# One-hot transposes of an attention and MLP kernel: both heads of a pair at once, 128 output rows in place of 64

## The chip, the cores and the metric

The kernel runs on one core of one Trainium2 chip. The metric is device time in microseconds (us) of one execution. Executions of the same kernel scatter by about 0.3 us and more, so most of what follows is read from traces, where the same instruction can be compared to within some 0.02 us.

## The reference, cut to what matters

Four batches of eight heads, 768 tokens, head size 64. Each query and key is assigned to the nearest of 16 centroids; a query attends to the keys of the same cluster only; then comes softmax, the product with v, and a GELU MLP.

```python
q_assign = np.argmax(np.einsum('bhsd,hcd->bhsc', q_n, c_n), axis=-1)
k_assign = np.argmax(np.einsum('bhsd,hcd->bhsc', k_n, c_n), axis=-1)
mask = q_assign[:, :, :, None] == k_assign[:, :, None, :]
scores = np.where(mask, scale * np.matmul(q, k.transpose(0, 1, 3, 2)), -1e9)
# softmax, then @ v;   x = that, heads side by side
# out = gelu(x @ w_in) @ w_out,  x: (3072, 512), w_in: (512, 2048)
```

## The kernel before

The mask enters the score product as 16 more rows of the contraction: the one-hot of the cluster (minus 1 on the key side, times a large number on the query side). So for each head the kernel needs q, k and both one-hots transposed. For heads 0 to 9 TensorE makes these transposes, for the later heads a DMA. In order, for one head: q transposes and their copy out by DVE, k transposes and copy, assignment products on TensorE, sum, maximum and comparison on DVE (the one-hot, [token, cluster]), one-hot transposes on TensorE, and two evictions by DVE into rows 64 to 79 of the transposed q and k.

```python
ps_sc = ...tile_pool(name="ps_sc", bufs=2, space=PSUM)   # scores
ps_a  = ...tile_pool(name="ps_a",  bufs=1, space=PSUM)   # assignment products
ps_x  = ...tile_pool(name="ps_x",  bufs=1, space=PSUM)   # attention times v
ps_o  = ...tile_pool(name="ps_o",  bufs=2, space=PSUM)   # all transposes of heads 0 to 9
# ... cut ...
ohs = [const.tile([128, N, 2, 2, 32], FP16, name=f"oh{t}") for t in range(NOH)]  # [token, chunk, head of pair, q/k, 32]
for t in ohs:
    nc.vector.memset(t[:, :, :, :, 16:32], 0.0)

def tr_pe(i, w, copy=None, pool=None):                  # w = 0: q, 1: k
    # ... cut ...
    for j in range(N):
        nc.tensor.transpose(t_ps[:, j * 128:(j + 1) * 128], st[:, w, j, :], ident)     # line 154
    (copy or nc.vector.tensor_copy)(Ts[i][:, w, :], t_ps)                              # line 155

def one_pe(i):
    oh = ohs[(i // 2) % NOH]
    e = i % 2
    t_ps = ps_o.tile([128, S], FP16, tag="op", name="oh_ps")
    for j in range(N):
        nc.tensor.transpose(t_ps[0:64, j * 128:(j + 1) * 128],
                            oh[:, j, e].rearrange("p b c -> p (b c)"), ident)          # line 265
    nc.vector.tensor_scalar(Ts[i][D:D + C, 1, :], t_ps[32:32 + C, :], -1.0, None, op0=ALU.add)          # 267
    nc.vector.tensor_scalar(Ts[i][D:D + C, 0, :], t_ps[0:C, :], float(VAL), None, op0=ALU.mult)         # 269
# ... cut: one_first, the same for head 0 in two halves (line 287) ...
AVS0 = {2: (0,), 3: (1, 2), 4: (3,), 5: (4, 5)}   # products with v after score chunk 2, 3, ...
def slot(i, c):                        # score chunk c of head i, c = 0 to 5
    scores(i, c)                       # 2 matmuls (line 311), 1 exponential on ACT (line 314)
    # ... products with v of head i-1 (line 326); after chunk 5 its normalization (336, 337)
# program order: g(i, c) is just after score chunk c of head i
        at(g(h - 2, 0), tr_pe, h, 0)
        at(g(h - 2, 2), tr_pe, h, 1)
        at(g(h - 2, 4), prep_asn, h, True)        # products 219, sum 232, maximum 239, one-hot 240
        at(g(h - 1, 1), one_pe, h)
    # x_tok of an even head and the next, transposed (350) and copied (352):
        at(g(h + 3, 3), fin, h, pe=True)
```

The pairs (i, c) show what shares a head's time: while head i is scored, head i+2 is transposed and assigned, and head i+1's one-hot is transposed.

The softmax here doesn't subtract the row's maximum and nothing guards it: scores larger than these inputs give would overflow.

## Time and profile before

| | before |
|---|---|
| time, median (range) of 3 runs | 302.98 us (302.97 to 303.14) |
| span of the profiled execution | 301.14 us |
| from the start to the first MLP product of line 386 (FC1 in the prediction) | 55.70 us |
| one pair of heads (two in a row, out of heads 3 to 7) | 9.71 us |

Three stages matter: a start of 8 us (loads, head 0), heads 0 to 9 with hardly any MLP work (eight products of one early tile), and from 55.7 us on a TensorE-bound rest of 245.4 us. The change touches the first two.

The page of the kernel before: busy time by engine, and the chain that ended last.

```profile
PE 296.4 (98%) x3109; PEld 186.0 (62%) x3109; DVE 121.7 (40%) x284; ACT 216.0 (72%) x274; POOL 106.8 (35%) x182
...
## 4 chain that ended last, share of the span: by engine, by line
PE 97%; ACT 1%; DVE 1%; issue 0%; DVEq 0%
```

The windows view over one pair of heads (28.66 to 38.37 us, from one sum on DVE to the same one two heads later); columns as in its first line.

```profile
core 0: us, PE busy (x) PEld busy (x) DVE busy (x) ACT busy (x) POOL busy (x), PEclk, DMA share, GB/s
28.66:38.37 9.71, 9.71 (x164) 7.51 (x163) 8.68 (x20) 9.29 (x13) 9.30 (x15) 1.00 1.17 266
```

PE is busy in all of it, then POOL, ACT, and DVE last. A matmul's busy time runs to its modelled end, which lies after the start of the next, so PE's 9.71 of 9.71 hides waits; they must be read from start-to-start distances. PE's row around one one-hot group (start us, us, engine, line, operation, out<-in, forms, count), in head 4:

```profile
29.86 0.49 PE L311 MATMUL sc_ps<-T 80*128 80x384 f16 x2
30.27 0.52 PE L265 MATMUL oh_ps<-ident,oh_167 128*64 128x128 f16 x6
30.73 0.50 PE L311 MATMUL sc_ps<-T 80*128 80x384 f16 x2
31.06 0.35 PE L326 MATMUL x_ps<-vaug_148,p_sb 128*128 128x65 f16 x6
31.25 0.50 PE L154 MATMUL tr_ps<-ident,st 128*128 128x128 f16 x6
```

`128*64` is the array form: 128 rows, 64 weight columns. The group starts 0.41 us after the first score matmul in front of it, where the plain sequence needs 0.16 (to the second score matmul) plus 0.16. Its weight loads, minimum/median/maximum ns, from the view of line 265:

```profile
L265 PEld LDWEIGHTS <-oh_166 x24: 106/110/110, 17.2 to 49.9; 128*64 128x64 f16 x24
```

DVE's row for the same head, from one one-hot to the next sum:

```profile
29.65 0.35 DVE L240 TENSOR_TENSOR oh_167<-asum,asn_ps 128x192 f16<-128x192 f32 x1
29.92 0.19 DVE L336 RECIPROCAL rec<-x_ps 128x6 f32<-128x6 f32 x1
30.14 0.56 DVE L337 TENSOR_TENSOR x_tok<-x_ps,rec 128x384 f16<-128x384 f32 x1
30.62 0.55 DVE L155 COPY T<-tr_ps 128x768 f16<-128x768 f16 x1
31.20 0.55 DVE L267 TENSOR_SCALAR T<-oh_ps 16x768 f16<-16x768 f16 x1
31.76 0.55 DVE L269 TENSOR_SCALAR T<-oh_ps 16x768 f16<-16x768 f16 x1
32.34 0.56 DVE L155 COPY T<-tr_ps 128x768 f16<-128x768 f16 x1
33.31 0.56 DVE L232 TENSOR_REDUCE asum<-asn_ps 128x192 f32<-128x384 f32 x1 [0.41 <-PE asn_ps L219]
```

In every second head, where x_tok is transposed as well, it looks like this (lines of both engines):

```profile
36.41 0.55 DVE L269 TENSOR_SCALAR T<-oh_ps 16x768 f16<-16x768 f16 x1
...
37.02 0.51 PE L350 MATMUL fin_ps<-ident,x_tok 128*128 128x128 f16 x6
...
37.88 0.45 PE L219 MATMUL asn_ps<-c_all,T 128*128 128x32 f16 x12
...
38.37 0.56 DVE L232 TENSOR_REDUCE asum<-asn_ps 128x192 f32<-128x384 f32 x1 [0.24 <-PE asn_ps L219]
```

And the clearing of the last one-hot buffer, with DVE's next instruction:

```profile
1.30 0.22 DVE L124 MEMSET oh_167<- 128x192 uint32 x1
3.26 0.36 DVE L162 CAST st<-q_raw 128x384 f16<-128x384 f32 x1 [1.75 <-DMA q_raw<-in_q_dram]
```

### The profile page before, as it was taken

The page shows a single profiled execution, that of the slowest core. Times are in us where ns is not written, and L with a number is a line of the kernel's source. Part 1 is how long each engine was busy: PE and PEld are TensorE (multiplying, and loading weights), DVE is VectorE, ACT ScalarE, POOL GpSimd, SP SyncE. Part 2 cuts the span into 40 slices and gives each one's busy share as a digit, 9 for nine tenths or more (in the row PEclk, how much of TensorE's full clock was granted, in tenths as well). Part 3 has the DMA queues.
Part 4 walks back from the last instruction along what each step waited for, and adds up shares of the span by engine and source line. Part 5 has one row for each costly group of instructions (what it writes and reads, how often), then busy time and mean ns, then how long its engine had stood idle before and what let it go on. Part 6 is the DMA issues. An engine that isn't in the chain of part 4 may idle for free.

```text
span 301.1 us, 7413 instructions
## 1 busy us (share of the span) xinstructions
PE 296.4 (98%) x3109; PEld 186.0 (62%) x3109; DVE 121.7 (40%) x284; ACT 216.0 (72%) x274; POOL 106.8 (35%) x182
## 2 busy tenths in 40 slices
PE   8899999999999999999999999999999999999996
PEld 4577777666666666666566666666566665565444
DVE  5788987103564742122353742213344413000112
ACT  5889999956888888856788888855788883466000
POOL 3999999997034104572633104600000000000000
PEclk9999999999999999999999999999999999999999
DMA  6999999994369348966679436876032242100122
GB/s 219 341 297 274 264 263 202 240 197 131 63 176 218 81 99 224 199 187 157 134 175 185 119 82 209 165 97 131 2 89 53 71 52 46 38 0 0 44 97 70
DMA packets 74065, 42.85 MB, mean 142 GB/s; under 512 B 54320, under 2 KB 71088, under 8 KB 74032
## 3 DMA queue, kind: packets, MB, share of 16 engines
q1 hardware_dynamic: 69520, 38.09, 53.4%
q0 software_dynamic: 4224, 4.19, 8.3%
q8 instruction: 24, 0.39, 0.5%
q10 hardware_dynamic: 288, 0.10, 0.1%
q14 instruction: 9, 0.07, 0.1%
HBM read 27.30 MB, written 6.29 MB: 112 GB/s over the span
## 4 chain that ended last, share of the span: by engine, by line
PE 97%; ACT 1%; DVE 1%; issue 0%; DVEq 0%
PE hp L386 27%; PE op L412 24%; PE sc_ps L311 21%; PE x_ps L326 11%; PE op_alt L412 3%; PE asn_ps L219 3%; PE tr_ps L154 2%; PE w_ps L98 1%; PE oh_ps L265 1%; ACT p_sb L314 1%; PE fin_ps L350 1%; PE asn_ps L223 0%; PE hp_early L367 0%; DVE T L269 0%; DVE T L267 0%
## 5 line engine op out<-in xcount | busy, mean ns | idle before, releaser
L314 ACT ACTIVATE p_sb<-sc_ps 128x768 f16<-128x768 f32 x192 | 149.7, 810 | 21.3 <-PE sc_ps L311 12.8
L311 PE MATMUL sc_ps<-T 80*128 80x384 f16 x384 | 93.8, 325 | 0.6 <-ACT p_sb L314 0.4
L386 PE MATMUL hp<-xt,w_in_sb 128*128 128x384 f16 x504 | 85.0, 326 | 0.0
L326 PEld LDWEIGHTS <-p_sb 128*128 128x128 f16 x1152 | 54.7, 97 | 30.8
L386 PEld LDWEIGHTS <-w_in_sb 128*128 128x128 f16 x504 | 47.9, 98 | 30.4
L132 POOL CAST st<-q_raw 128x384 f16<-128x384 f32 x30 | 15.4, 513 | 78.9 <-DMA q_raw<-in_q_dram 57.3
L416 DVE COPY o_sb<-op 128x512 f32<-128x512 f32 (+1 forms) x22 | 14.8, 672 | 55.0 <-PE op L412 54.9
L232 DVE TENSOR_REDUCE asum<-asn_ps 128x192 f32<-128x384 f32 x29 | 16.2, 558 | 50.8 <-PE asn_ps L219 50.7
L311 PEld LDWEIGHTS <-T 80*128 80x128 f16 x384 | 26.2, 97 | 5.8 <-issue 0.9
L133 POOL TENSOR_TENSOR st<-q_raw,st 128x384 f16<-128x384 f32 x30 | 27.3, 911 | 2.4
L135 POOL TENSOR_TENSOR st<-k_raw,st 128x384 f16<-128x384 f32 x30 | 27.4, 912 | 2.4
L336 DVE RECIPROCAL rec<-x_ps 128x6 f32<-128x6 f32 x32 | 6.2, 193 | 43.8 <-PE x_ps L326 43.8
L337 DVE TENSOR_TENSOR x_tok<-x_ps,rec 128x384 f16<-128x384 f32 x32 | 17.8, 558 | 1.1
L219 PEld LDWEIGHTS <-T 128*128 128x128 f16 x348 | 14.6, 96 | 4.4
L219 PE MATMUL asn_ps<-c_all,T 128*128 128x32 f16 x348 | 16.5, 177 | 0.0
L134 POOL CAST st<-k_raw 128x384 f16<-128x384 f32 x30 | 15.1, 505 | 0.0
L275 DVE TENSOR_SCALAR T<-ohT 16x768 f16<-16x768 f16 x22 | 7.9, 361 | 8.0 <-DMA ohT<-oh_166 3.6
L239 DVE TENSOR_REDUCE asn_ps<-asum 128x12 f32<-128x192 f32 x29 | 10.5, 361 | 1.0
L154 PE MATMUL tr_ps<-ident,st 128*128 128x128 f16 x120 | 10.6, 228 | 0.2 <-DVE T L269 0.2
L154 PEld LDWEIGHTS <-st 128*128 128x128 f16 x120 | 8.2, 101 | 2.9 <-DVE st L163 0.8
L155 DVE COPY T<-tr_ps 128x768 f16<-128x768 f16 x17 | 9.4, 554 | 0.6
L278 DVE TENSOR_SCALAR T<-ohT 16x768 f16<-16x768 f16 x22 | 8.6, 391 | 0.3
(308 smaller groups left out, 404.8 us busy)
## 6 DMA issues: line engine op xcount, KB each, us to landing
q_raw<-in_q_dram SPq DMA_DIRECT2D x32, 192.0 KB, 4.1
k_raw<-in_k_dram SPq DMA_DIRECT2D x32, 192.0 KB, 4.1
v_raw<-in_v_dram SPq DMA_DIRECT2D x32, 192.0 KB, 4.4
out_dram<-o_sb SPq DMA_DIRECT2D x23, 256.0 KB, 2.2
w_in_sb<-in_moe_w_in_dram POOLq DMA_DIRECT2D x4, 512.0 KB, 10.4
w_out_sb<-in_moe_w_out_dram POOLq DMA_DIRECT2D x4, 512.0 KB, 11.9
T<-st SPq DMA_TRANSPOSE x22, 4.9
xt<-x_tok SPq DMA_TRANSPOSE x11, 2.9
```

The costliest lines, as they stand in the source:

```text
L132: nc.gpsimd.tensor_copy(st[:, 0, :, 0:D], q_raw)
L133: nc.gpsimd.tensor_sub(st[:, 0, :, D:2 * D], q_raw, st[:, 0, :, 0:D])
L135: keng.tensor_sub(st[:, 1, :, D:2 * D], k_raw, st[:, 1, :, 0:D])
L154: nc.tensor.transpose(t_ps[:, j * 128:(j + 1) * 128], st[:, w, j, :], ident)
L219: nc.tensor.matmul(a_ps[:, j, which], t[:, js], c_all[:, :, chs], start=True, stop=True)
L232: nc.vector.tensor_reduce(out=asum, in_=a_ps.rearrange("p n w l c -> p n w c l"), axis=AX.X, op=ALU.add)
L311: nc.tensor.matmul(s_ps[:, t, 0:QB], Ts[i][0:D + C, 1, c * 128:(c + 1) * 128], Ts[i][0:D + C, 0, t * QB:(t + 1) * QB], start=True, stop=True)
L314: nc.scalar.activation(ps[i][:, c, :].rearrange("p (t q) -> p t q", t=2), s_ps[:, :, 0:QB], ACT_FN.Exp, bias=0.0, scale=float(scale))
L326: nc.tensor.matmul(x_ps[:, j], ps[i][:, ch, j * 128:(j + 1) * 128], va[:, ch, 0:D + 1], start=(ch == 0), stop=(ch == N - 1))
L337: nc.vector.tensor_tensor(xtoks[i - i % 2][:, :, i % 2, :], x_ps[:, :, 0:D], rec.to_broadcast([128, N, D]), op=ALU.mult)
L386: nc.tensor.matmul(hp[:, t, 0:QB], w_in_sb[:, m, f * 128:(f + 1) * 128], xts[b][:, m, t * QB:(t + 1) * QB], start=(m == 0), stop=(m == NM ...
L412: nc.tensor.matmul(op[:, 0:w], gs[b][f][:, js], w_out_sb[:, f, ms], start=(f == 0), stop=(f == NF - 1))
```

## The change

Its intent: weight loads and transposes of 64 columns put TensorE in another array form and back, ten times. With both heads of the pair taken at once the form stays 128x128. The other head's rows are computed and not read, so its buffer must hold something: the clearing covers all of it.

```diff
-        nc.vector.memset(t[:, :, :, :, 16:32], 0.0)
+        nc.vector.memset(t, 0.0)
@@ one_pe
-            nc.tensor.transpose(t_ps[0:64, j * 128:(j + 1) * 128],
-                                oh[:, j, e].rearrange("p b c -> p (b c)"), ident)
-        nc.vector.tensor_scalar(Ts[i][D:D + C, 1, :], t_ps[32:32 + C, :],
+            nc.tensor.transpose(t_ps[:, j * 128:(j + 1) * 128],
+                                oh[:, j].rearrange("p a b c -> p (a b c)"), ident)
+        nc.vector.tensor_scalar(Ts[i][D:D + C, 1, :], t_ps[64 * e + 32:64 * e + 32 + C, :],
                                 -1.0, None, op0=ALU.add)
-        nc.vector.tensor_scalar(Ts[i][D:D + C, 0, :], t_ps[0:C, :],
+        nc.vector.tensor_scalar(Ts[i][D:D + C, 0, :], t_ps[64 * e:64 * e + C, :],
                                 float(VAL), None, op0=ALU.mult)
# ... cut: the same two lines for head 0
```

More of the change, by code (lines that the diff above doesn't have):

```diff
@@ L286, in one_first @@
             for j in range(N // 2):
-                nc.tensor.transpose(t_ps[0:64, j * 128:(j + 1) * 128],
-                                    ohs[0][:, e * (N // 2) + j, 0].rearrange("p b c -> p (b c)"),
+                nc.tensor.transpose(t_ps[:, j * 128:(j + 1) * 128],
+                                    ohs[0][:, e * (N // 2) + j].rearrange("p a b c -> p (a b c)"),
                                     ident)
```

## The prediction

> **What bounds the kernel.** The page's chain that ended last is 97% PE; PE is busy 98%, ACT 72%, DVE 40%. The affected stage is the first 56 us (heads 0 to 9); after it the chain is pure PE, so an earlier start should pass through one to one. In the first stage PE and ACT take turns. By the windows view, between 20 and 55 us ACT is busy 4.6 to 4.9 of each 5 us, PE 4.8 to 5.0. Exponentials back to back start 0.70 us apart (0.805 us each, overlapping 0.10), so ACT alone would need 4.2 us a head; the heads take 4.65 (no x_tok transpose) or 5.06 us (with one). Most steps wait for PE; one, the second score chunk of each head, waits for ACT (it starts 0.05 us after the exponential two before it ends).
>
> **What the change does.** No instruction is added or removed; order and semaphore waits stay. Ten groups of six one-hot transposes go from a 128x64 to a 128x128 array form. The matmuls stream the same 128 columns: 56 ns apart inside a group, as the 128x128 transposes of q and k (line 154), so the doubled output rows are free. The load of 64 weight columns takes 110 ns, that of 128 columns 97 to 101. What goes is at the edges. Start-to-start distances, one-hot group against line-154 group:
> - last score matmul to first transpose: 253 ns against 161;
> - first to second transpose: 80 against 55 to 59;
> - last transpose to next matmul: 152 against 56;
> - first to second score matmul after it: 173 against 162 to 167.
> That is about 0.21 us a group, 1.9 us over nine. The Trainium skill, "TensorEngine Tiling (Array Packing)", Key Properties, says that changing the tiling mode drains TensorE, and under Restrictions that column tiling disables fast weight load; both fit (line-154 weight loads start before the previous matmul is through, those of the one-hots only with their matmul).
>
> The memsets of the three one-hot buffers write twice the elements (0.22 us each before; I estimate 0.3 to 0.45) and end by about 2.1 us; DVE then waits for q_raw until 3.26: hidden. The evictions read the same 16 rows at another partition: no change.
>
> **How much is on the path.** The group follows chunk 1 of a head; chunk 2's scores wait for the exponential of chunk 0. They start 162 to 169 ns after it ends; the floor seen elsewhere is 51. So heads 4 to 8 give only about 0.115 each, not 0.21: 0.58. Head 2's group has 0.7 us of room: 0.20. Head 3: 0.14 (it waits for the one-hot, mainly the exit counts). Head 1: 0.11, through DVE's wait for it. Head 9: 0.06, chunk 3 already waits for ACT. Head 0: 0.03. Sum about 1.1 us.
>
> **Prediction:** 302.98 - 1.1 = 301.9 us, 301.2 to 302.6 eight times in ten. Faster by over 2%: 0.5%; within 2%: 99%; slower: 0.5%.
>
> **What would show it.** One-hot groups as 128*128, weight loads near 100 ns; entry near 161, exit near 56 ns or longer where it waits for ACT; chunk 2's scores 51 ns after the exponential; head pairs at 9.47 us instead of 9.70; FC1 starting at about 54.7 us instead of 55.86, everything later shifted equally. Memsets longer, still done before q_raw lands.
>
> **What would make it wrong.** If the edges come not from the array form but from waits on DVE or the PSUM buffer, nothing is gained (302.9). If ACT's floor moves too, up to 1.9 us (301.1). If a later stage is paced by a DMA or POOL (95% busy until 67 us), the gain is given back there.

## More of the kernel before

Every run was with a granted TensorE clock of 1.0 or 0.999.

From 29.65 to 32.90 us DVE goes from instruction to instruction without a wait, and takes up the one-hot transposes (line 267) at 31.20, while PE had started the last of them at 30.58 (30.27 plus 0.08 plus four times 0.056). Then comes one gap of 0.41 us before line 232.

## The result, and the profile after

| | before | after |
|---|---|---|
| first measurement, median (range) | 303.00 us (302.97 to 303.14), 4 runs | 302.75 us (302.68 to 302.94), 4 runs |
| its ratio | | 0.9992, 95% interval 0.9975 to 1.0009 |
| second measurement | 302.95 us (302.90 to 303.46), 9 runs | 302.95 us (302.62 to 303.13), 5 runs |
| its ratio | | 0.9995, 95% interval 0.9983 to 1.0008 |

A ratio is the mean time of one kernel's runs over that of the other's of the same rounds, so not quite the ratio of the medians. Both intervals hold 1: end to end, the gain of 0.0 to 0.25 us is not clear of the noise. The traces are clearer. From the first exponential to the end the kernel before takes 291.25 us, the changed one 291.03 and 290.99 in two profiles: 0.23 to 0.26 us less. The 1.1 us forecast did not come.

The same views after. The page:

```profile
PE 295.8 (98%) x3109; PEld 186.8 (62%) x3109; DVE 122.8 (41%) x284; ACT 215.2 (72%) x274; POOL 106.6 (35%) x182
...
## 4 chain that ended last, share of the span: by engine, by line
PE 94%; POOL 2%; DVE 1%; ACT 1%; issue 0%
```

One pair of heads (28.50 to 38.23 us, the same two sums):

```profile
28.50:38.23 9.73, 9.73 (x164) 7.86 (x163) 8.70 (x20) 9.07 (x13) 9.32 (x15) 1.00 1.16 255
```

PE around the same group, and the weight loads:

```profile
29.70 0.48 PE L311 MATMUL sc_ps<-T 80*128 80x384 f16 x2
30.02 0.50 PE L265 MATMUL oh_ps<-ident,oh_167 128*128 128x128 f16 x6
30.45 0.48 PE L311 MATMUL sc_ps<-T 80*128 80x384 f16 x2
30.78 0.34 PE L326 MATMUL x_ps<-vaug_148,p_sb 128*128 128x65 f16 x6
31.06 0.49 PE L154 MATMUL tr_ps<-ident,st 128*128 128x128 f16 x6
```

```profile
L265 PEld LDWEIGHTS <-oh_166 x24: 95/97/100, 17.1 to 49.7; 128*128 128x128 f16 x24
```

The form is now `128*128`, and the edges that the prediction named are gone, except the exit: from the last transpose to the next score matmul it is 150 ns, was 152, and this is now a wait for an exponential. First score matmul to first one-hot transpose: 0.32 us, was 0.41. But look at the last line of this view, before and after: from the start of the products with v (line 326) to the k transposes (line 154) it took 0.19 us before and takes 0.28 now. PE arrives earlier and waits. What for is in DVE's row:

```profile
30.46 0.55 DVE L155 COPY T<-tr_ps 128x768 f16<-128x768 f16 x1
31.04 0.56 DVE L267 TENSOR_SCALAR T<-oh_ps 16x768 f16<-16x768 f16 x1
31.62 0.56 DVE L269 TENSOR_SCALAR T<-oh_ps 16x768 f16<-16x768 f16 x1
32.20 0.56 DVE L155 COPY T<-tr_ps 128x768 f16<-128x768 f16 x1
33.17 0.56 DVE L232 TENSOR_REDUCE asum<-asn_ps 128x192 f32<-128x384 f32 x1 [0.41 <-PE asn_ps L219]
```

Line for line it is the row of before, shifted by 0.14 to 0.16 us: the copy of q, the two evictions, the copy of k, and the same gap of 0.41 us. DVE's copy of q (line 155) ends at 31.012 us, and PE's k transposes, which need its buffer, start 0.05 us later. Before, it ended at 31.165 and PE came 0.085 us later: PE had 0.035 us to spare there. The pair of heads takes 9.73 us, was 9.71.

In the head with x_tok, too, the rows follow each other as before, the x_tok transposes right after the end of the second eviction (36.82 us here, 36.96 before):

```profile
36.27 0.55 DVE L269 TENSOR_SCALAR T<-oh_ps 16x768 f16<-16x768 f16 x1
36.88 0.51 PE L350 MATMUL fin_ps<-ident,x_tok 128*128 128x128 f16 x6
...
38.23 0.56 DVE L232 TENSOR_REDUCE asum<-asn_ps 128x192 f32<-128x384 f32 x1 [0.24 <-PE asn_ps L219]
```

A ledger from the traces, in us, each stretch between the starts of two exponentials (3.0 is chunk 0 of head 3) or from there to the first MLP product of line 386:

| stretch | before | after | after, second profile |
|---|---|---|---|
| start to head 0's one-hot | 8.171 | 8.225 | 8.112 |
| 0.0 to 2.0 | 9.905 | 9.587 | 9.583 |
| 2.0 to 3.0 | 4.906 | 5.026 | 5.026 |
| 3.0 to 8.0 | 24.465 | 24.503 | 24.482 |
| 8.0 to 9.2 | 5.919 | 5.848 | 5.855 |
| 9.2 to the first MLP product | 0.618 | 0.633 | 0.633 |
| from there to the end | 245.441 | 245.429 | 245.411 |

The gain is made in heads 0 and 1 (0.32), a part is given back in head 2 (0.12), heads 3 to 7 give nothing, and heads 8 and 9 give 0.07. The first of these repeats in all profiles: 9.905 to 9.913 us in the six kernels with 64 columns in heads 0 to 2, 9.583 to 9.590 in the nine with 128.

What PE's time became, in the pair of heads 5 and 6: summing what the start-to-start distances exceed the normal ones (0.162 us for 384 columns streamed, 0.056 for 128, 0.029 for 65, 0.025 for 32), before there were 0.44 us of edges of the one-hot groups among 0.78 us in all; after there are no such edges and 0.80 us in all, of which 0.25 are waits for exponentials (0.06 before) and 0.22 waits before the k transposes (none before). The edges turned into waits.

The clearing takes longer and is hidden, as forecast:

```profile
1.73 0.38 DVE L124 MEMSET oh_167<- 128x384 uint32 x1
3.33 0.36 DVE L162 CAST st<-q_raw 128x384 f16<-128x384 f32 x1 [1.22 <-DMA q_raw<-in_q_dram]
```

### The profile page after: what moved, and what is told of

Read it like the earlier page. It is cut to its first block, busy times and chain, and to the rows that moved or that the text cites. A ratio compares the mean times of both kernels' runs of the same rounds, so it can differ in the third digit from the quotient of the medians.

```text
span 300.9 us, 7413 instructions
## 1 busy us (share of the span) xinstructions
PE 295.8 (98%) x3109; PEld 186.8 (62%) x3109; DVE 122.8 (41%) x284; ACT 215.2 (72%) x274; POOL 106.6 (35%) x182
## 4 chain that ended last, share of the span: by engine, by line
PE 94%; POOL 2%; DVE 1%; ACT 1%; issue 0%
PE hp L386 27%; PE op L412 24%; PE sc_ps L311 20%; PE x_ps L326 11%; PE op_alt L412 3%; PE asn_ps L219 3%; PE tr_ps L154 2%; PE w_ps L98 1%; PE oh_ps L265 1%; PE fin_ps L350 1%; POOL st L133 1%; ACT p_sb L314 1%; ACT T L155 1%; PE hp_early L367 0%; POOL st L132 0%; POOL st L135 0%
## 5 line engine op out<-in xcount | busy, mean ns | idle before, releaser
L275 DVE TENSOR_SCALAR T<-ohT 16x768 f16<-16x768 f16 x22 | 8.2, 371 | 8.2 <-DMA ohT<-oh_166 4.0
L278 DVE TENSOR_SCALAR T<-ohT 16x768 f16<-16x768 f16 x22 | 9.0, 410 | 0.3
```

## The experiments

Theory A: in heads 3 to 8 DVE, taking its instructions in order, and PE release each other in a loop that the one-hot group is not part of. Rival B: the prediction's own mechanism, the exponentials on ACT as the floor, only mis-sized. The times below are device times; "3.0 to 8.0" is the stretch of the ledger, 24.465 us in the kernel before and 24.48 to 24.50 in the changed one. All results were accepted as correct.

### w0to2: the change for heads 0 to 2 alone

```diff
+        wide = i < 3          # else as before, in 64 columns
```

> The change for heads 0, 1 and 2 alone (all three buffers cleared whole as in the change). Theory A (in heads 3 to 8 DVE, working through its instructions in order, sets the pace, and the one-hot group on PE is not in that loop): nearly the whole gain of the change remains, 302.70 to 302.80 us; in the trace the start of the q/k transposes is 0.15 to 0.18 us earlier than in the kernel before from head 3 on and stays so to head 8 (no loss per pair, because the evictions of the odd heads read from the low partitions again); a pair of heads 9.70 us. Rival B (ACT's exponentials absorb what PE gains, as the prediction's floor says, and only the size is off): less gain than the whole change, because heads 3 to 9 are missing, with the shift growing from head to head in the changed kernel and not here.

Measured: 302.98 us median (302.57 to 303.16), ratio 0.9994 (0.9980 to 1.0008). The time missed the range: in this profile head 0's one-hot came at 8.46 us, 0.29 later than before, in the start that the change hardly touches. From the first exponential to the end it took 291.01 us, 0.24 less than before, which is the whole gain of the full change; 3.0 to 8.0 took 24.454. As theory A has it.

### w3to9: the change for heads 3 to 9 alone

```diff
+        wide = i >= 3         # head 0 in 64 columns too
```

> The change for heads 3 to 9 alone. Theory A: no gain in heads 3 to 8 although each of their groups is 0.2 us shorter on PE: 302.9 to 303.05 us; the q/k transposes shift by 0 from head 3 and then 0.016 us later with every odd head (its two evictions from the high partitions take 10 and 6 ns longer); a pair of heads 9.70 to 9.72 us; PE's gaps before the second q/k group of each head about 0.10 us longer. The prediction on record would have 302.1 to 302.3 here.

Measured: 302.97 us median (302.88 to 303.73), ratio 1.0003 (0.9991 to 1.0016). 3.0 to 8.0 took 24.491 us, 0.026 more than before, although five groups in it are shorter on PE. From the first exponential to the end 291.21 us, 0.05 less, which heads 8 and 9 gave (5.849 against 5.919). This alone rules out the 0.58 us that were predicted for the groups of heads 4 to 8, which lie in this stretch.

### b_nosum and a_nosum: DVE's sum left out for heads 3 to 9, in both kernels

A wrong result (the maximum that follows goes to SBUF and no longer to PSUM, cut here): the cluster is chosen from the high halves of the centroids alone, so 0.558 us a head of DVE go and PE's work stays.

```diff
-            asum = small.tile(...); nc.vector.tensor_reduce(out=asum, in_=..., op=ALU.add)
+            if i < 10:
+                asum = a_ps[:, :, :, 0, :]
```

> Kernel before, but for heads 3 to 9 the one-hot is made from the high halves alone: the sum of the two halves on DVE (0.558 us a head) is left out. Wrong result on purpose (a few assignments flip), same PE work. Theory A: DVE stops pacing; PE is left with its own work and the mode switches: a pair of heads 9.50 to 9.60 us instead of 9.70, total 302.4 to 302.7 us. Rival B: pair stays 9.70, total 303.0.

> The changed kernel with the same omission on DVE, wrong result on purpose. Theory A: now the shorter one-hot groups count: a pair of heads 9.30 to 9.40 us, total 301.5 to 301.9 us, that is 0.7 to 1.0 us under the same omission in the kernel before (the change as such gave 0.25). Rival B: as the changed kernel, 302.75, and no more apart from the other than 0.25.

Measured: 302.52 us (302.24 to 302.86), ratio 0.9982 (0.9970 to 0.9995), and 301.10 us (301.00 to 301.44), ratio 0.9938 (0.9926 to 0.9951). A pair of heads takes 9.57 and 9.31 us, both as expected. With DVE out of the way the change is worth 1.17 us from the first exponential to the end (290.57 against 289.40), where it gave 0.23 in the original kernel; the total of a_nosum is under its range (301.5 to 301.9), so the total difference, 1.42 us, is over the 0.7 to 1.0 expected. Over heads 3 to 7 it is 24.090 less 23.432 us, 0.13 a head, near the 0.115 of the prediction: once DVE is out of the way, the exponentials do take their part of the 0.2 us (in a_nosum the exit of the group takes 149 ns, where 56 would do). But rival B, which had both kernels unchanged here, falls: ACT is not what held the gain back.

### after2: the changed kernel again

> The changed kernel once more, for a tighter ratio and a second profile. Theory A: 302.6 to 302.9 us, that is 0.1 to 0.3 under the kernel before. In the trace the stretch from the first exponential of head 3 to that of head 8 takes 24.50 us as in its first profile (24.47 before), heads 0 to 2 together 0.2 us less than before, and FC1 to the end 245.4 us as before; the start up to head 0's one-hot, which was 8.17, 8.23, 8.46 and 8.12 us in four profiles, differs by 0.1 to 0.3 for no reason of the kernel's.

Measured: as in the tables above. The median is 0.05 us over the range expected; the ledger repeats to 0.02 us apart from the start.

### a_dveplus: one more small DVE instruction a head

```diff
+        if 4 <= i <= 8:                  # after the two evictions of one_pe
+            nc.vector.memset(dz, 0.0)    # scratch tile, 128 x 128 fp16
```

> The changed kernel with one small extra DVE instruction (a 128x128 fp16 memset of a scratch tile, estimated at 0.1 to 0.14 us with its gap from the memsets seen) after the one-hot evictions of heads 4 to 8, that is once in each of the heads 3 to 7. Theory A: each head gets longer by the whole instruction, so head 3 to head 8 takes 25.0 to 25.2 us instead of 24.50, and the total rises by as much. Rival B (PE and ACT set the pace, DVE has slack): no change, 24.50 us; PE waits 0.2 us a head there in any case.

Measured: 303.53 us (303.02 to 304.04), ratio 1.0017 (1.0002 to 1.0032); in this profile the start was 0.34 to 0.45 us later than in the changed kernel's two. 3.0 to 8.0 took 24.852 us, 0.36 more, which is under the range expected, and the heads say why. DVE in a head without x_tok (the new instruction is line 273, all lines are moved by one to three):

```profile
31.95 0.56 DVE L270 TENSOR_SCALAR T<-oh_ps 16x768 f16<-16x768 f16 x1
32.58 0.11 DVE L273 MEMSET dz<- 128x64 uint32 x1
32.73 0.56 DVE L156 COPY T<-tr_ps 128x768 f16<-128x768 f16 x1
33.69 0.56 DVE L233 TENSOR_REDUCE asum<-asn_ps 128x192 f32<-128x384 f32 x1 [0.41 <-PE asn_ps L220]
```

From the end of the eviction to the end of the copy of k it takes 0.78 us here and 0.59 without the memset; the head takes 4.849 us and not 4.664. So 0.19 us more on DVE are 0.19 us more for the head, one to one. PE shows the link: just before the assignment products of k it waited 0.06 us in the changed kernel and waits 0.25 here. In the heads with x_tok the copy started before the memset's reported end and its end moved by 0.01 us only; those heads stayed at 5.06. The dose did not arrive there, so they show nothing.

### b_order and a_order: k transposes and assignment products one score chunk earlier, one-hot transposes one later

```diff
-            at(g(h - 2, 2), tr_pe, h, 1)          -> g(h - 2, 1)      (h > 3)
-            at(g(h - 2, 4), prep_asn, h, h > 2)   -> g(h - 2, 3)
-            at(g(h - 1, 1), one_pe, h)            -> g(h - 1, 2)      (3 <= h <= 8)
```

> Kernel before, with the order changed for heads 3 to 9: the k transposes come one score chunk earlier than the one-hot transposes and not one later, and the assignment products one chunk earlier, so that DVE does not wait for PE's assignment products after the copy of k and PE not for DVE's copies. Correct result. Theory A: DVE stops pacing, PE does, with the mode switches in it: a pair of heads 9.50 to 9.65 us as without the sum (9.57), total 302.3 to 302.7. Rival B: nothing.

> The changed kernel in the same new order, correct result. Theory A: the shorter one-hot groups now count: a pair of heads 9.30 to 9.45 us, total 301.2 to 301.9, that is 0.6 to 1.2 under the new order alone and better than both kernels. Rival B: within 0.3 of the new order alone.

Measured: 304.50 us (304.08 to 304.80), ratio 1.0049 (1.0036 to 1.0062), and 302.71 us (302.63 to 302.95), ratio 0.9991 (0.9978 to 1.0004). Both expectations failed: the order is no improvement. In a_order PE waits three times a head for exponentials (0.18, 0.04 and 0.08 us beyond the normal distances). What the pair does show: here the one-hot group is on the path, and the change is worth 25.445 less 24.335 us over five heads, 0.222 a head, the 0.21 us that the prediction read from the edges.

### a_split and b_split: DVE's order, and the x_tok transposes one score chunk later

```diff
 # one_pe, heads 3 to 8: eviction to k-side rows at once; eviction to q-side rows
 # after the copy of k:   at(g(h - 1, 2) + 0.001, one_rest, h)
-            at(g(h + 3, 3) if h < 6 else g(9, 1), fin, h, pe=True)
+            at(g(h + 3, 4) if h < 6 else g(9, 1), fin, h, pe=True)
```

> The changed kernel with DVE's order changed and PE's nearly kept: for heads 3 to 8 the second one-hot eviction comes after the copy of k instead of before it, so that PE's assignment products run beside it, and the x_tok transposes come after the assignment products. Correct result. Theory A (DVE's own order, with its wait for the assignment products, sets the pace in heads 3 to 8): DVE's gap of 0.41 us before the sum falls to under 0.1, heads without x_tok take 4.45 to 4.55 us instead of 4.66, those with it 4.80 to 4.90 instead of 5.05; head 3 to head 8 23.4 to 23.9 us instead of 24.48; total 301.2 to 302.1. Rival B: head 3 to head 8 stays at 24.4 to 24.5.

> The kernel before in the same new DVE order. Theory A: with DVE's gap gone PE sets the pace, with the mode switches in it: head 3 to head 8 24.0 to 24.3 us instead of 24.47, total 302.3 to 302.7; so the one-hot groups' form is worth 0.5 to 1.2 us in this order where it gave 0.2 in the old one. Rival B: 24.4 to 24.5 and no more between the two than 0.3.

Measured: 302.51 us (302.40 to 302.77), ratio 0.9983 (0.9971 to 0.9996), and 302.76 us (302.67 to 303.13), ratio 0.9994 (0.9981 to 1.0008). 3.0 to 8.0 took 24.181 and 24.282 us: the first missed its range, the second is at the edge of it, both totals are above theirs, and the two differ by 0.10 where 0.5 to 1.2 were expected. DVE in a_split, in a head without x_tok (line 278 is the eviction that was moved):

```profile
30.52 0.55 DVE L155 COPY T<-tr_ps 128x768 f16<-128x768 f16 x1
31.10 0.56 DVE L267 TENSOR_SCALAR T<-oh_ps 16x768 f16<-16x768 f16 x1
31.70 0.56 DVE L155 COPY T<-tr_ps 128x768 f16<-128x768 f16 x1
32.29 0.56 DVE L278 TENSOR_SCALAR T<-oh_ps 16x768 f16<-16x768 f16 x1
33.16 0.56 DVE L232 TENSOR_REDUCE asum<-asn_ps 128x192 f32<-128x384 f32 x1 [0.32 <-PE asn_ps L219]
```

The eviction now stands where the gap was, but a gap of 0.32 us is left. PE waited 0.23 and 0.10 us before the k transposes, for the copy of q in the first of these lines, so everything behind them, the assignment products included, came late. This suggested another leg of the loop: the pool of two buffers.

### a_order2 and b_order2: the early order, with PE's work spread evenly

```diff
+            av3 = {2: (0,), 3: (), 4: (1, 2, 3), 5: (4, 5)} if i % 2 else \
+                {2: (0,), 3: (1,), 4: (2, 3), 5: (4, 5)}      # for heads 2 to 7, in place of AVS0
```

> The order that failed (a_order), with the attention products spread so that PE has about the same work between any two score chunks of heads 2 to 7. In a_order PE waited three times a head (0.31 us) for exponentials while ACT idled elsewhere, since chunks 0 to 2 had little PE work and chunks 3 and 4 much. If that unevenness is why it failed: head 3 to head 8 23.2 to 23.9 us instead of 24.34, total 301.0 to 302.0. If DVE still sets the pace there: 24.2 to 24.4.

> The kernel before in the order of a_order2 (the best so far, 301.69 us with the changed transposes), so with the 64-column transposes. Theory A: in this order PE sets the pace, so the mode switches cost their full 0.2 us a head: head 3 to head 8 24.2 to 24.55 us against 23.43, heads 0 to 2 again 0.3 us longer, total 302.6 to 303.2; the change is then worth 0.9 to 1.5 us where it gave 0.2 in the original order. If the order alone made a_order2 fast: 301.8 to 302.1.

Measured: 301.69 us (301.42 to 301.89), ratio 0.9954 (0.9940 to 0.9967), and 303.07 us (303.05 to 303.60), ratio 1.0002 (0.9990 to 1.0015). 3.0 to 8.0 took 23.426 and 24.535 us, both as expected. So the unevenness was what spoiled a_order, and in this correct kernel the change is worth 1.109 us over five heads, 0.222 each, and 1.4 us in the medians. The order alone brings nothing and the change alone next to nothing; together they bring 1.4 us.

### a_split_psa: a_split, with the k transposes in the bank of the assignment products

```diff
-            at(g(h - 2, 2), tr_pe, h, 1)
+            at(g(h - 2, 2), tr_pe, h, 1, pool=(ps_a, "asn") if h > 3 else None)
```

> a_split with one thing more: the k transposes of heads 4 to 9 go to the bank of the assignment products (free then) instead of the pool of two in which they wait for DVE's copy of q. Theory A with a second leg (DVE's copy of q frees the buffer, PE then does the k transposes, two score chunks and the assignment products, for which DVE waits): PE's waits of 0.10 and 0.23 us before the k transposes go, DVE's gap before the sum falls from 0.32 to under 0.15, head 3 to head 8 23.4 to 23.8 us instead of 24.18, total 301.3 to 302.0. If this buffer is not the leg: 24.1 to 24.2 and 302.5.

Measured: 301.31 us (301.29 to 301.63), ratio 0.9940 (0.9926 to 0.9953): 1.8 us under the kernel before in the medians, and the best correct kernel. (This order was not run with the 64-column transposes, so how much of the 1.8 us is the change is not known here.) 3.0 to 8.0 took 23.431 us. PE's waits before the k transposes are gone. DVE, in a head without x_tok:

```profile
30.00 0.55 DVE L155 COPY T<-tr_ps 128x768 f16<-128x768 f16 x1
30.58 0.56 DVE L267 TENSOR_SCALAR T<-oh_ps 16x768 f16<-16x768 f16 x1
31.17 0.56 DVE L155 COPY T<-tr_ps 128x768 f16<-128x768 f16 x1
31.76 0.56 DVE L278 TENSOR_SCALAR T<-oh_ps 16x768 f16<-16x768 f16 x1
32.40 0.56 DVE L232 TENSOR_REDUCE asum<-asn_ps 128x192 f32<-128x384 f32 x1
```

The sum now follows the eviction after 0.085 us (0.22 in heads with x_tok), and no wait is listed. The buffer was the second leg.

## Why the prediction was wrong

Right, point by point:
- The array form is what made the edges. Entry 161 ns was measured as 162, the second transpose after 58, the score matmuls after it 162 apart. The exit is 148 to 150 ns in the groups of heads 4 to 9, because chunk 2 now waits for the exponential of chunk 0 and starts 51 ns after it, as forecast. The Trainium skill, "TensorEngine Tiling (Array Packing)", Key Properties, says that a change of tiling mode drains TensorE; the trace fits this, and gives the amount of one excursion as a whole, 0.22 us. It does not separate the drain from the weight loads, which in the 64-column form start only with their matmul.
- The doubled output rows are free, the weight loads get shorter (97 ns for 110), the clearing is hidden (it ends at 2.11 us, q_raw's conversion starts at 3.33), and what is gained before 55 us passes to the end unchanged (245.4 us in every kernel).
- The groups of heads 1 and 2: forecast 0.31 us, measured 0.32 (stretch 0.0 to 2.0). There DVE did wait for the one-hot transposes, 0.87 and 0.59 us, and now waits 0.76 and 0.48. Head 9's group: forecast 0.06, measured 0.07 (stretch 8.0 to 9.2).

Wrong: the step "Most steps wait for PE; one, the second score chunk of each head, waits for ACT", and from it "So heads 4 to 8 give only about 0.115 each". They gave nothing: 24.465 us became 24.48 to 24.50.

The same step failed for "Head 3: 0.14", whose group lies in head 2: the stretch 2.0 to 3.0 became 0.12 us longer. Head 3's group is not the reason for that, since w0to2, which leaves it in 64 columns, has 5.007 us there, and w3to9, which changes it and no group in front of it, 4.920 (4.906 before). Head 2 too hangs on DVE: without DVE's sum it takes 4.48 (a_nosum) and 4.62 us (b_nosum), so what heads 0 and 1 gain is partly waited away there. These two terms, forecast at 0.58 and 0.14, and the 0.12 lost are the missing part of the 1.1 us.

The prediction weighed PE against ACT and never asked about DVE, which the windows view had as the least busy of four. What paces heads 3 to 7 is a loop through DVE and parts of PE:
1. DVE works through its instructions in order without a wait, from the sum to the copy of k (in DVE's row of before, 29.65 to 32.90 us). Then PE makes the assignment products of k, for which that copy must be there, and DVE waits for these. a_dveplus shows this leg: 0.19 us on DVE is 0.19 us on the head.
2. DVE's copy of q frees the buffer in which PE makes the k transposes; two score chunks and the assignment products stand behind them. a_split against a_split_psa shows this one: with leg 1 relaxed and leg 2 kept, 24.18 us; with both relaxed, 23.43. Leg 2 relaxed alone was not run.
3. In heads with x_tok the end of the second eviction (36.96) lets PE's x_tok transposes begin at 37.02, and the assignment products come behind them. This is read from the trace; no run tried it alone (a_split moved it together with leg 1).

The one-hot group lies in none of them: its result is ready about 0.4 us before DVE, busy with other things, takes it up. A faster group makes PE arrive earlier at the k transposes, where it may gain 0.035 us and then waits for DVE.

POOL, as busy as ACT here, is a rival that no run tested, but the traces settle it: POOL runs ahead. It was done with the inputs of head 8's k transposes at 34.7 us both in the kernel before and in a_split_psa, while PE took them up at 40.95 and 39.68.

The Trainium skill, "Perfetto Trace Analysis", Identifying the Most-Contended Engine, ranks VectorE, ScalarE and GpSimd by occupancy. Here that points the wrong way: over a pair of heads POOL has 9.30 us of 9.71, ACT 9.29, DVE 8.68, and it is DVE's order that paces. The same page, Optimization Strategy, says that the same gap coming back again and again can mean that buffers are lacking; the trace agrees, as a_split_psa shows, though the gap was on DVE and the lacking buffer in front of PE.

A small loss was not foreseen either (the prediction: "no change"). In the changed kernel the evictions of odd heads read PSUM from partition 96 or 64 on, and take 561 to 562 and 554 to 555 ns. Those of the even heads, behind the same 128-row transposes but from partition 32 or 0, take 551 to 552 and 548 to 549, as all did in the kernel before, to within 1 ns (heads 1 to 9). That is 0.016 us per odd head on the engine that paces: 9.73 for 9.71 a pair. With it kept at the low partitions, w0to2, heads 3 to 7 took 24.454 us.

Open: the start. Head 0's one-hot came between 8.12 and 8.22 us in the five profiles with the short clearing, and between 8.11 and 8.56 in the ten with the long one. The three latest all have the long one, but DVE was idle for at least 1.2 us after it, and in w0to2 (8.46) DVE is where it was in the changed kernel (8.23) up to 5.56 us; the delay first shows in PE's centroid transposes, 6.22 for 6.04. What causes it is not known. And three kernels (a_nosum, a_order2, a_split_psa) all take 23.43 us for 3.0 to 8.0: PE there waits 0.03 and 0.09 us a head for exponentials, so PE and ACT together set that floor, but this was not tested.

## What to carry to other kernels

Before costing a saving on one engine, follow the result of the shortened work: if its consumer takes it up long after it is ready, the saving is off the path, however busy the engine looks. Look for the next thing that the freed engine will wait for, and read its slack as a time (here 0.035 us), above all where a pool of two buffers or another engine's program order stands in between. A change that gives nothing may be worth its whole size once the order is right: here 0.2 us in the old order, and 1.4 us in a new one that alone gave nothing.

## What the Trainium skill lacked or had wrong

- "TensorEngine Tiling (Array Packing)", Key Properties, names the drain at a mode switch but no cost. Here one excursion from 128x128 to 128x64 and back cost 91 ns on entry, 24 at the second transpose, 96 on exit and 11 after it, 0.22 us together (drain and later weight loads not separated); 0.222 us a head where it was on the path.
- "TensorE: Matmul & The Clock Gate", LDWEIGHTS: the formula of columns over 1.2 gives 53 ns for 64 columns and 107 for 128. The profile has durations of 106 to 110 ns for 64 columns and 95 to 100 for 128. These durations overlap and are no load rate (128-column loads of line 219 start 25 ns apart), so they do not refute the formula as a rate. The page's section on fast weight load lets one expect that 128 columns are faster than the formula, but neither says that halving the columns makes the recorded load longer.
- The same page, Part 4: PE-mode transpose, has transposes at about 275 ns in a kernel, without the full clock. Here those of a group mostly follow each other every 55 to 56 ns at a granted clock of 1.0, with a modelled duration of 219 ns. They stand among other matmuls, so what clock transposes alone would get is not shown.
- "Perfetto Trace Analysis", Identifying the Most-Contended Engine: occupancy alone would have named POOL or ACT. It lacks the case of two engines that release each other through program order and a pool of two buffers, where neither is saturated (DVE 8.68 us of 9.71; PE with 0.78 us beyond its normal start-to-start distances).
- I found on none of the pages that evictions from PSUM at partition 64 or 96 take longer: 562 against 552 ns and 555 against 549.
